# Contiguous first loads and a token-major, woven end in an attention and ReGLU kernel

## The chip, the cores and the metric

The kernel runs on one core of a Trainium2 chip. The metric is device time in microseconds. Runs of one kernel scatter by about 1 us here. So times are compared as means of several runs taken in the same rounds, and the traces are read beside them.

## The reference

Two parts in a row, four batches, 49152 tokens of 128 channels:

```python
# attention with spatially reduced keys, which are also the values
kv_pool = kv.reshape(B, H//4, 4, W//4, 4, C).mean(axis=(2, 4))   # 384x32 pixels -> 768 keys
k = v = kv_pool.reshape(B, -1, C) @ w_sr
x = softmax(q @ k.T / sqrt(C)) @ v                               # B = 4, 12288 queries each
# ReGLU: d_model 128, d_ff 1536
out = (maximum(x @ w_gate, 0) * (x @ w_val)) @ w_out
```

## The kernel before

It works in 96 tiles of 512 tokens, four tiles to a group. Per tile there are 6 score matmuls, 24 value matmuls of 129 columns, and 12 hidden blocks, each with a value, a gate and an output projection. TensorE (PE) does all of these; ScalarE (ACT) does the exponentials and copies the value projections; VectorE (DVE) multiplies gate and value into the hidden block `hT`. The output projection of tile k-4 runs beside the scores of tile k.

The parts that the change touches (cuts are marked with `# ...`):

```python
def q_load_plain(i0, i1):                    # called for (0, 2) and (2, 4), tiles of group 0
    q32 = work.tile([128, i1 - i0, NS, C], FP32, ...)
    nc.sync.dma_start(
        q32, q[0, 0 : GRP * T, :].rearrange("(p i s) c -> p i s c", p=128, i=GRP)[:, i0:i1]
    )
# ...
def out_proj(k, fb):
    if k == NT - 2:                          # token-major: hT is the stationary operand
        # ... four matmuls of 128 columns, one for each slice s of 128 tokens
        return
    nc.tensor.matmul(o_banks[k], wo16[:, fb, :], hTs[k][:, fb, :], ...)   # one of 512 columns

def out_turn(k):                             # channel-major result: turned in 32x32 blocks
    nc.vector.transpose(o_t, o_banks.pop(k))
    nc.gpsimd.tensor_scalar(o_sb..., o_t..., 1.0 / X_SCALE**2, None, op0=ALU.mult)
    # ... 4 stores of 64 KB for a tile; 16 of 16 KB in the first and the last group

def out_last(k):                             # the last tile, token-major
    o_ps = bank([128, 2, 128])
    for s in range(2):
        for fb in range(NFB - 1):
            out_add(k, fb, s, o_ps[:, s], fb == 0 and s == 0)
    for s in range(2):
        out_add(k, NFB - 1, s, o_ps[:, s], False)
    out_scale(k, nc.vector, slice(0, 2), o_ps)
    out_store(k, slice(0, 2))
    for s in range(2, NS):
        o_ps = bank([128, 1, 128])
        for fb in range(NFB):
            out_add(k, fb, s, o_ps[:, 0], fb == 0)
        out_scale(k, (nc.scalar, nc.vector)[s % 2], slice(s, s + 1), o_ps)
    out_store(k, slice(2, NS))
```

The kv of the first batch (three pairs of key chunks, 2 MB each, each pair in four loads or lines of 512 KB) and q's first megabyte come through one queue, SyncE's (SPq): one kv pair, the two loads of q, then two kv pairs.

The softmax here doesn't subtract the row's maximum and nothing guards it: scores larger than these inputs give would overflow.

## Time and profile before

| | before |
|---|---|
| time, median of 3 runs | 1035.74 us (1035.46 to 1036.62) |
| span in the profile | 1034.1 us |
| PE busy | 1023.5 us, 99% |
| value projections start (end of the start-up) | 30.92 us |
| last scale done | 1029.48 us |
| last store issued, landed | 1030.44, 1032.78 us |

The prediction below shows the lines. Two habits help in reading them. A PE row of 99% says that the middle of the run is full, so the two ends are to be looked at one microsecond at a time. And a transfer's "landing" is read in this text from the trace's completion counts: a transfer is shared by the 16 DMA engines, each of which reports once, and the landing is the sixteenth report (for kv's fourth line, in the trace of before, the first report came at 8.61 us and the sixteenth at 9.71).

### The profile page before, as it was taken

What the parts mean: (1) busy time and instruction counts of PE and PEld (TensorE: products, weight loads), DVE (VectorE), ACT (ScalarE), POOL (GpSimd) and SP (SyncE); (2) the same over time, 40 slices, a digit from 0 to 9 for tenths busy, and PEclk for the clock granted to TensorE, in tenths of its full rate; (3) what the DMA queues carried; (4) which work ended last, traced back from release to release, by engine and by line L of the source; (5) the groups of instructions that cost most, each with busy time, mean ns of one, the idle gap of its engine ahead of it and who ended that gap; (6) DMA issues with size and microseconds to landing.
All of it is one profiled execution on the core that took longest, in us unless ns stands there. A gap on an engine that the chain in (4) does not pass through costs nothing.

```text
span 1034.1 us, 19981 instructions
## 1 busy us (share of the span) xinstructions
PE 1023.5 (99%) x6540; PEld 543.3 (53%) x6540; DVE 910.6 (88%) x1669; ACT 909.6 (88%) x1749; POOL 281.4 (27%) x288
## 2 busy tenths in 40 slices
PE   8999999999999999999999999999999999999998
PEld 5555555555555555555555555555555555555554
DVE  3888889998989898998889898989898989888897
ACT  4988899888888889888888888888898888889986
POOL 1212146521211125642212121664121211111111
PEclk9999999999999999999999999999999999999999
DMA  8936396562543547736345157573652533513122
GB/s 292 133 57 74 84 198 144 83 92 43 82 67 50 80 120 161 169 53 89 55 64 88 31 86 151 142 161 57 82 78 42 78 60 56 86 31 67 31 46 48
DMA packets 330840, 93.34 MB, mean 90 GB/s; under 512 B 310768, under 2 KB 324080, under 8 KB 330736
## 3 DMA queue, kind: packets, MB, share of 16 engines
q1 hardware_dynamic: 315648, 78.76, 39.1%
q0 software_dynamic: 14944, 13.24, 10.6%
q8 instruction: 51, 0.84, 0.3%
q14 instruction: 53, 0.43, 0.2%
q10 hardware_dynamic: 144, 0.07, 0.0%
HBM read 53.94 MB, written 26.35 MB: 78 GB/s over the span
## 4 chain that ended last, share of the span: by engine, by line
PE 97%; DMA 2%; DVE 0%; SPq 0%; ACT 0%; issue 0%
PE bank_ps L278 24%; PE bank_ps L289 24%; PE bank_ps L313 24%; PE bank_ps L240 12%; PE bank_ps L229 12%; DMA parts<-in_kv_dram 1%; DMA q<-in_q_dram 1%; PE bank_ps L299 0%; PE bank_ps L188 0%; DVE hT L292 0%; SPq L138 0%; ACT aT L230 0%; PE bank_ps L162 0%; PE bank_ps L180 0%; SPq L100 0%
## 5 line engine op out<-in xcount | busy, mean ns | idle before, releaser
L292 DVE SCALAR_TENSOR_TENSOR hT<-bank_ps,val 128x512 f16<-128x512 f32 x1152 | 758.2, 686 | 91.6 <-ACT val L282 71.1
L282 ACT CAST val<-bank_ps 128x512 f16<-128x512 f32 x1152 | 678.7, 591 | 102.4 <-PE bank_ps L278 100.5
L278 PE MATMUL bank_ps<-xT,wv 128*128 128x512 f16 x1152 | 436.6, 379 | 0.1
L289 PE MATMUL bank_ps<-xT,wg 128*128 128x512 f16 x1152 | 436.6, 379 | 0.0
L313 PE MATMUL bank_ps<-hT,wo 128*128 128x512 f16 x1128 | 427.5, 379 | 0.0
L230 ACT ACTIVATE aT<-bank_ps 128x512 f16<-128x512 f32 x576 | 346.3, 605 | 0.9 <-PE bank_ps L229 0.8
L323 POOL TENSOR_SCALAR o_sb<-o_t 128x512 f32<-128x512 f32 x94 | 140.0, 1489 | 700.8 <-DVE rinv L248 673.3
L240 PEld LDWEIGHTS <-aT 128*128 128x128 f16 x2304 | 177.2, 98 | 133.4 <-issue 0.9
L240 PE MATMUL bank_ps<-kv,aT 128*128 128x129 f16 x2304 | 223.5, 220 | 0.5 <-DVE kv L198 0.4
L229 PE MATMUL bank_ps<-qT,kv 128*128 128x512 f16 x576 | 216.8, 379 | 0.4 <-DVE qT L121 0.2
L278 PEld LDWEIGHTS <-wv 128*128 128x128 f16 x1152 | 112.7, 98 | 133.6 <-issue 0.2
L289 PEld LDWEIGHTS <-wg 128*128 128x128 f16 x1152 | 112.7, 98 | 68.6 <-issue 0.2
L313 PEld LDWEIGHTS <-wo 128*128 128x128 f16 x1128 | 110.4, 98 | 67.2
L229 PEld LDWEIGHTS <-kv 128*128 128x128 f16 x576 | 56.1, 98 | 68.0 <-ACT kv L182 0.8
L256 DVE TENSOR_TENSOR x<-bank_ps,rinv 128x256 f16<-128x256 f32 x188 | 79.7, 425 | 6.6
L321 DVE STREAM_TRANSPOSE o_t<-bank_ps 128x512 f32<-128x512 f32 x94 | 66.4, 706 | 0.0
L85 POOL DMA_DIRECT2D q<-in_q_dram x88 | 48.4, 557 | 0.3 <-issue 0.3
L147 POOL TENSOR_TENSOR s<-parts 128x512 f32<-128x512 f32 x36 | 44.9, 1266 | 0.0
L248 DVE RECIPROCAL rinv<-bank_ps 128x2 f32<-128x2 f32 x192 | 28.0, 146 | 0.6 <-PE bank_ps L240 0.6
L149 POOL TENSOR_TENSOR s<-s 128x512 f32<-128x512 f32 x18 | 22.8, 1269 | 1.4
L151 POOL TENSOR_TENSOR c<-s 128x256 f32<-128x256 f32 x18 | 13.1, 728 | 1.4
L173 ACT COPY kvT<-bank_ps 128x128 f32<-128x128 f32 x4 | 1.1, 266 | 11.2 <-PE bank_ps L162 9.7
(53 smaller groups left out, 94.4 us busy)
## 6 DMA issues: line engine op xcount, KB each, us to landing
parts<-in_kv_dram SPq DMA_DIRECT2D x48, 512.0 KB, 6.6
out_dram<-o_sb SPq DMA_DIRECT2D x352, 64.0 KB, 2.2
q<-in_q_dram POOLq DMA_DIRECT2D x88, 128.0 KB, 4.4
out_dram<-o_sb SPq DMA_DIRECT2D x96, 16.0 KB, 1.5
xT<-x SPq DMA_TRANSPOSE x94, 2.4
placed<-blocks SPq DMA_DIRECT2D x9, 128.0 KB, 1.8
kvT<-placed SPq DMA_DIRECT2D x36, 32.0 KB, 1.9
q<-in_q_dram SPq DMA_DIRECT2D x2, 512.0 KB, 8.3
```

Source lines behind the costliest of these rows:

```text
L85: nc.gpsimd.dma_start(q16[32 * j : 32 * (j + 1)].rearrange("t (i s) c -> t i s c", i=GRP), rows[j])
L229: nc.tensor.matmul(s_ps, kv16[:, k // NST, jc, 0:C], qT_of(k), start=True, stop=True)
L230: nc.scalar.activation(aTs[k][:, jc, :], s_ps, AF.Exp, scale=qk_scale)
L240: nc.tensor.matmul(x_ps[:, i, :], aTs[k][:, jc, s * 128 : (s + 1) * 128], kv16[:, k // NST, jc, C : 2 * C + 1], start=(jc == 0 and i == 0) ...
L256: nc.vector.tensor_tensor(x16s[k][:, 2 * half : 2 * half + 2, :], x_ps[:, :, 0:C], rinv.to_broadcast([128, 2, C]), op=ALU.mult,)
L278: nc.tensor.matmul(va_ps, wv16[:, fb * 128 : (fb + 1) * 128], xTs[k], start=True, stop=True)
L282: nc.scalar.copy(val, va_ps)
L289: nc.tensor.matmul(g_ps, wg16[:, fb * 128 : (fb + 1) * 128], xTs[k], start=True, stop=True)
L292: nc.vector.scalar_tensor_tensor(hTs[k][:, fb, :], g_ps, 0.0, vals.pop((k, fb)), op0=ALU.max, op1=ALU.mult)
L313: nc.tensor.matmul(o_banks[k], wo16[:, fb, :], hTs[k][:, fb, :], start=fb == 0, stop=fb == NFB - 1)
L321: nc.vector.transpose(o_t, o_banks.pop(k))
L323: nc.gpsimd.tensor_scalar(o_sb.rearrange("t j s c -> t s j c"), o_t.rearrange("t (s j c) -> t s j c", s=NS, j=4), 1.0 / X_SCALE**2, None, ...
```

## The change

Its intent: read the first queries as two contiguous half megabytes instead of as interleaved 4 KB pieces, and shorten the end. "Token-major" means that a tile's result comes out with the tokens on the partitions, so it needs no turning and leaves in one store of 256 KB instead of sixteen of 16 KB. "Woven" means that the last tile's matmuls go through its four slices of 128 tokens in a mixed order, so that the first slices can be scaled and stored while the last are computed. Since the load then gives partition p the eight tokens 8p to 8p+7 of its half megabyte, the stores of the first four tiles get new addresses, in the same number and sizes.

```diff
-            q32, q[0, 0 : GRP * T, :].rearrange("(p i s) c -> p i s c", p=128, i=GRP)[:, i0:i1]
+            q32, q[0, i0 * T : i1 * T, :].rearrange("(p i s) c -> p i s c", i=i1 - i0, s=NS)
@@ out_proj
-        if k == NT - 2:
+        if k >= NT - 3:
@@ out_turn
-            if g in (0, NG - 1):
+            if g == 0:
+                to = rows.rearrange(
+                    "(e j t i s) (b c) -> e b i j t s c", e=2, j=4, t=32, s=NS, c=32
+                )
+                moves += [(to[k // 2, b, k % 2, j], o_b[:, j]) for j in range(4)]
+            elif g == NG - 1:
@@ out_last, whole body
+        parts = [bank([128, 2, 128]), bank([128, 1, 128]), bank([128, 1, 128])]
+        owns = [slice(0, 2), slice(2, 3), slice(3, 4)]
...   add(s, a, b): blocks a to b-1 of slice s; keep(n, engine): scale part n, then store it
+        held = NFB - 1
+        add(0, 0, held)
+        add(1, 0, held)
+        add(2, 0, held - 4)
+        add(0, held, NFB)
+        add(1, held, NFB)
+        keep(0, nc.vector)
+        add(2, held - 4, NFB)
+        keep(1, nc.scalar)
+        add(3, 0, NFB)
+        keep(2, nc.vector)
@@ main loop
-                if step == NFB - 1 and k < last:
+                if step == NFB - 1 and kO < NT - 3:
                     out_moves = out_turn(kO)
+                elif step == NFB - 1 and k < last:
+                    out_scale(kO, nc.vector, slice(0, NS))
+                    out_store(kO, slice(0, NS))
```

(A condition on group 0 in another load, which is never called for it, is left out.)

More of the change, by code (lines that the diff above doesn't have):

```diff
@@ L79, in q_load @@
         rows = q[b, n0 : n0 + GRP * T, :]
-        if g in (0, NG - 1):
+        if g == NG - 1:
             nc.gpsimd.dma_start(q16, rows.rearrange("(p s) c -> p s c", p=128))
@@ L333, in out_turn @@
             o_b = o_sb[32 * b : 32 * (b + 1)]
-            if g in (0, NG - 1):
+            if g == 0:
[4 more added lines that the diff above has]
+            elif g == NG - 1:
                 to = rows.rearrange("(j t i s) (b c) -> b i j t s c", j=4, t=32, s=NS, c=32)
@@ L361, in out_last, with add, keep @@
     def out_last(k):
+        parts = [bank([128, 2, 128]), bank([128, 1, 128]), bank([128, 1, 128])]
+        owns = [slice(0, 2), slice(2, 3), slice(3, 4)]
         o_banks[k] = None
-        o_ps = bank([128, 2, 128])
-        for s in range(2):
-            for fb in range(NFB - 1):
-                out_add(k, fb, s, o_ps[:, s], fb == 0 and s == 0)
-        for s in range(2):
-            out_add(k, NFB - 1, s, o_ps[:, s], False)
-        out_scale(k, nc.vector, slice(0, 2), o_ps)
-        out_store(k, slice(0, 2))
-        for s in range(2, NS):
-            o_ps = bank([128, 1, 128])
-            for fb in range(NFB):
-                out_add(k, fb, s, o_ps[:, 0], fb == 0)
-            out_scale(k, (nc.scalar, nc.vector)[s % 2], slice(s, s + 1), o_ps)
-        out_store(k, slice(2, NS))
+        def add(s, fb0, fb1):
+            n = max(s - 1, 0)
+            for fb in range(fb0, fb1):
+                out_add(k, fb, s, parts[n][:, s - owns[n].start], fb == 0 and s != 1)
+        def keep(n, engine):
+            out_scale(k, engine, owns[n], parts[n])
+            out_store(k, owns[n])
+        held = NFB - 1
[9 more added lines that the diff above has]
+        keep(2, nc.vector)
     ctx.enter_context(tc.manual_schedule())
```

## The prediction

> **What bounds the kernel now.** I read the page first, then the chain of waits, then the timelines of the first 35 us and the last 25 us, engine by engine. The page settles where a gain cannot come from:
>
> ```profile
> PE 1023.5 (99%) x6540; PEld 543.3 (53%) x6540; DVE 910.6 (88%) x1669; ACT 909.6 (88%) x1749; POOL 281.4 (27%) x288
> ...
> PE 97%; DMA 2%; DVE 0%; SPq 0%; ACT 0%; issue 0%
> ```
>
> TensorE (PE) is 99% busy and is 97% of the chain that ended last. In the middle, a pair of steps (six matmuls of 512 columns, one more for the scores, four of 129) takes 1.74 us, again and again. The change touches none of those matmuls. What is left to win lies at the two ends: before about 31 us, where PE waits for data, and after the last hidden block, where the result is written out.
>
> The start, in the chain of waits (start us, length us, what):
>
> ```profile
> 4.07 8.63 DMA q<-in_q_dram
> 12.69 0.02 issue
> 12.71 11.67 DMA parts<-in_kv_dram
> 24.38 0.14 issue
> 24.52 1.50 PE bank_ps L162 x12
> ```
>
> PE's work at 24.52 waits for the last line of kv. The stream before it is 2 MB of kv, 1 MB of q (the two loads that change), 4 MB of kv, all in one queue. By stretches of 1 us (columns: length, busy of five engines, clock, DMA share, GB/s):
>
> ```profile
> 7.00:8.00 1.00, 0.70 (x7) 0.46 (x5) 0.00 (x0) 0.00 (x0) 0.00 (x0) 1.00 1.06 340
> 8.00:9.00 1.00, 0.49 (x5) 0.50 (x6) 0.00 (x0) 0.00 (x0) 0.00 (x0) 1.00 1.01 324
> 9.00:10.00 1.00, 0.85 (x8) 0.61 (x7) 0.00 (x0) 0.00 (x0) 0.00 (x0) 1.00 1.00 287
> 10.00:11.00 1.00, 1.00 (x9) 0.82 (x8) 0.29 (x1) 0.12 (x1) 0.00 (x0) 1.00 0.98 336
> 11.00:12.00 1.00, 0.69 (x5) 0.39 (x4) 0.62 (x2) 0.42 (x3) 0.00 (x0) 1.00 1.03 422
> ```
>
> The DMA engines are busy throughout (share about 1), but move only 287 to 340 GB/s from 7 to 11 us and 422 after. The packets of 4096 bytes take 159 ns each when all is well and 189 to 228 ns on average in those four slices.
>
> The end, in the timelines of the store queue (SPq), PE and VectorE (DVE):
>
> ```profile
> 1019.96 9.43 SPq L535 DMA_DIRECT2D out_dram<-o_sb  x18
> 1029.49 1.35 SPq L352 DMA_DIRECT2D out_dram<-o_sb  x3
> ```
> ```profile
> 1025.92 0.72 PE L299 MATMUL bank_ps<-wo,hT 128*128 128x128 f16 x10
> 1026.86 2.30 PE L299 MATMUL bank_ps<-wo,hT 128*128 128x128 f16 x38 [0.21 <-DVE hT L292]
> ```
> ```profile
> 1019.57 7.83 DVE L292 SCALAR_TENSOR_TENSOR hT<-bank_ps,val 128x512 f16<-128x512 f32 x13
> 1027.91 0.42 DVE L349 TENSOR_SCALAR o_sb<-bank_ps 128x256 f32<-128x256 f32 x1 [0.51 <-PE bank_ps L299]
> 1029.19 0.29 DVE L349 TENSOR_SCALAR o_sb<-bank_ps 128x128 f32<-128x128 f32 x1 [0.86 <-PE bank_ps L299]
> ```
>
> The reader should see that the queue is still sending the small stores of the third last tile until 1029.39. The second last tile is ready at about 1027.0 and the first half of the last at 1028.33, yet all three large stores go out in a row from 1029.49. The last is issued at 1030.44, though its data was ready at 1029.48, and its completion count is full at 1032.78. The span ends at 1034.1.
>
> **What the Trainium skill says.** "DMA: Bandwidth & Descriptors", Rules for kernel authors, advises to coalesce small transfers. This trace agrees, in the queue's time: a 16 KB store holds the queue for 0.43 us and comes every 0.47, a 256 KB store of one piece to a partition holds it for 0.38. The same page, Latency and other measured facts, says that a row pitch of large powers of two (512 KiB and more) slows a copy, and infers channel aliasing. The pitch of q was 8 KiB and becomes 4, far below those; and the trace speaks against a penalty here: of the two loads of q, both with 8 KiB pitch, the first landed 1.70 us after the transfer before it, the second 1.28, and undisturbed kv loads of the same 512 KB land every 1.27 to 1.28. "TensorE: Matmul & The Clock Gate", on sustained spacing, gives about 81 ns for a matmul of 128 columns with its weight load; this trace has four in 0.22 us, 56 ns each, so I use that.
>
> **The change, part by part.**
>
> *Loads of q.* Each stays 128 pieces of 4096 bytes; only addresses change (tiles 0 and 1 from the first half megabyte, 2 and 3 from the second). The most there is to win: 4 us at 422 would have moved 1688 KB, 1287 came, so 401 KB or 0.95 us. But the dip starts at 7.2 us, when (by the completion counts) no DMA engine has reached q yet, and the second load of q is at full speed. What q itself shows is 1.70 - 1.28 = 0.42 us. I count 0.35 us, about that, partly discounted for the doubt and partly raised by a share of the dip before it. Would it reach the end? PE's start at 24.52 needs kv lines that landed at 23.14 and 24.38; each was held up by one DMA engine out of sixteen (the other fifteen were through at 21.65 and 22.89), on which an instruction fetch of 16 KB took 1.1 us from 20.98. Both move with what comes before, so I pass the 0.35 on in full. From 31 us PE is the bound and hands it on.
>
> *Third last tile token-major.* Removed: 12 matmuls of 512 columns, one VectorE transpose (0.71 us busy, 0.63 to the next instruction), one GpSimd scale (1.49, off the path), 16 stores. Added: 48 matmuls of 128 columns, one VectorE scale of 128x512, one store. PE: four small ones take 0.225 against 0.216, as the second last tile already shows with a step of 0.655 against 0.645; 12 steps, +0.1 us. It is hidden, since VectorE runs without a gap from 1011.8 to 1027.4 and sets when the last hidden blocks come. The scale: 0.42 us for 256 columns and 0.29 for 128, so 0.13 per 128 more, 0.69 for 512, against 0.71. Net on the path about -0.02. The queue: 16 stores are gone, from 1021.2 to 1029.4, so it stands free when the large ones come. This is the main gain.
>
> *Last tile woven, three stores.* PE stops at the 11th hidden block (the 10 matmuls at 1025.92, then a wait to 1026.86). In the new order the first run is again 11 blocks of slice 0, so it stops at the same place, and 1 + 11 + 7 + 2 + 5 + 12 = 38 matmuls follow, the same 38 as now. The weave wins PE nothing. It moves the ends: with 56 ns spacing and 0.22 for one, slices 0 and 1 are done after 21 matmuls (1028.2, now 1027.7), slice 2 after 26 (1028.5), slice 3 after 38 (1029.16, as now). Then: scale of the pair to 1028.65, store issued 1028.65 to 1029.03; scale of slice 2 on ScalarE to 1028.85, store to 1029.45; scale of slice 3 to 1029.48, store issued at 1029.5, which is 0.95 us earlier than 1030.44.
>
> *Landing of the last store.* Now 2.34 us from issue (1030.44 to 1032.78), behind 512 KB put in within a microsecond, at 316 to 393 GB/s. Then 64 KB, with only 192 KB near it. Yardsticks: the 16 KB stores land 1.5 us after issue, the 64 KB load of w_sr 1.8 (0.73 to 2.51). I take 1.8: 1029.5 + 1.8 = 1031.3, against 1032.78. Gain 1.5 us in all.
>
> *The stores of the first four tiles* keep their number and size; they are in mid-run behind PE: 0.
>
> Sum: -0.35 (start) - 1.5 (end) = -1.85. 1035.74 - 1.85 = **1033.9 us**.
>
> **The rivals.** (1) The start gives nothing, because the dip belongs to the time and not to the addresses: for it speaks the full-speed second half of q at the same pitch, and the slow packets before any q. Then about 1034.2. (2) The dip is q's alone and the whole 0.95 us comes back: for it, the dip ends as the first q load does. Then about 1033.3. The fetch on one engine could also fall elsewhere, worth up to 1.2 us either way (fifteen engines against the sixteenth); VectorE's adds and the kvT copies would eat part of it. (3) The end is eaten by a new wait: the scale of the third last tile now shares the three store buffers with the transposed tiles, and VectorE in the middle of its full stretch waits for stores of tile 90. Against it: those were issued some 20 us earlier. Or the bundle of three banks for the last tile waits for a reader; the order of instructions shows only waits for ScalarE and VectorE steps long over. If one bites, some 0.5 us is lost: 1034.4. (4) VectorE becomes more loaded: by its row lengths it does not.
>
> **Range and chances.** Start between -0.95 and +0.2, end between -1.1 and -1.8, the run-to-run spread of before 1.2 us (1035.46 to 1036.62). An eighty per cent range is 1032.9 to 1035.0. Two per cent is 20.7 us, which neither end has to give or take: same 0.99, and 0.005 to either side.
>
> **What would show it.** The small stores (now 32 of 16 KB after 1013) are 16, over by about 1021; five large stores, issued near 1020, 1027, 1028.7, 1029.1 and 1029.5 on the old clock, the last straight after its scale. PE has 38 matmuls after its stop at the 11th block. From the end of the last scale to the end of the span: 4.6 us now, 3.1 then. The q rows: first load landing 1.3 us after kv's fourth if addresses were the cause, still 1.7 if not; the first continuous PE stretch starting 0 to 0.9 us before 30.9. Wrong it would be if the last store still left late, if 64 KB took over 2.3 us to land, or if the start moved later.

## The result, and the profile after

| | before | after |
|---|---|---|
| time, median of 6 runs each | 1036.08 us | 1034.02 us (1032.81 to 1034.72) |
| mean of the same 6 runs | 1036.06 us | 1033.81 us |
| ratio | | 0.9978, 95% interval 0.9965 to 0.9991 |
| span in the profile | 1034.1 us | 1031.3 us |
| value projections start | 30.92 us | 29.69 us |
| last scale done | 1029.48 us | 1028.25 us |
| last store issued, landed | 1030.44, 1032.78 us | 1028.43, 1030.15 us |

A ratio is the mean time of one kernel's fast runs over that of the other's fast runs of the same rounds, so not quite the ratio of the two medians. It is by 2.1 to 2.3 us faster.

Lines have moved by some numbers in the file after: L279 is the value projection, L290 the gate, L300 the small output matmuls, L355 and L358 the scale and the store. The start, by the same stretches of 1 us as in the prediction (columns: length, busy of five engines, clock, DMA share, GB/s):

```profile
7.00:8.00 1.00, 0.78 (x8) 0.54 (x5) 0.00 (x0) 0.00 (x0) 0.00 (x0) 1.00 1.03 401
8.00:9.00 1.00, 0.55 (x5) 0.55 (x6) 0.00 (x0) 0.00 (x0) 0.00 (x0) 1.00 1.02 373
9.00:10.00 1.00, 0.83 (x9) 0.60 (x7) 0.00 (x0) 0.00 (x0) 0.00 (x0) 1.00 1.02 414
10.00:11.00 1.00, 1.00 (x10) 0.82 (x8) 0.29 (x1) 0.16 (x1) 0.00 (x0) 1.00 1.00 410
```

Where before moved 287 and 336 GB/s from 9 to 11 us, after moves 414 and 410. (From 7 to 9 us the traces of the study overlap, 332 to 379 GB/s with the old loads and 365 to 420 with the contiguous ones, so the difference seen there is not credited to the change.) The chain of waits (start, length, what) around 23 us has no DMA in it in this trace:

```profile
22.27 0.61 PE bank_ps L241 x8
22.89 0.43 PE bank_ps L230 x2
23.32 1.47 PE bank_ps L163 x12
```

PE goes from the scores straight on to the transposes of the last kv lines (L163), which before waited for a transfer until 24.38. Not every execution does: in the second trace of the changed kernel (after_again) PE waits 0.69 us for a kv line there, until 23.77.

The end, in the timeline of the store queue and in the chain of waits:

```profile
1019.23 1.41 SPq L553 DMA_DIRECT2D out_dram<-o_sb  x1
1020.74 8.09 SPq L358 DMA_DIRECT2D out_dram<-o_sb  x5
```
```profile
1024.36 0.53 issue
1024.89 0.69 DVE hT L293
1025.63 2.31 PE bank_ps L300 x38
1027.96 0.29 DVE o_sb L355
```

The small stores are over at 1020.64, and the five large ones go out at 1020.74, 1025.88, 1027.53, 1027.95 and 1028.43: the first as soon as the small ones are through, the next two as their data come, and the last two 0.33 and 0.18 us after theirs, each behind the store before it. PE still stops before the 11th hidden block, and still has 38 matmuls after the stop, in 2.31 us as before. From the end of the last scale to the end of the span it is 3.05 us (1028.25 to 1031.3), where it was 4.6.

### The profile page after: what moved, and what is told of

The parts are those of the page before. It is cut to its first block, busy times and chain, and to the rows that moved or that the text cites. A ratio compares the mean times of both kernels' runs of the same rounds, so it can differ in the third digit from the quotient of the medians.

```text
span 1031.3 us, 20034 instructions
## 1 busy us (share of the span) xinstructions
PE 1023.6 (99%) x6576; PEld 545.2 (53%) x6576; DVE 910.4 (88%) x1669; ACT 909.6 (88%) x1749; POOL 279.9 (27%) x287
## 4 chain that ended last, share of the span: by engine, by line
PE 98%; DMA 1%; ACT 0%; DVE 0%; SPq 0%; issue 0%
PE bank_ps L279 24%; PE bank_ps L290 24%; PE bank_ps L314 23%; PE bank_ps L241 13%; PE bank_ps L230 12%; DMA parts<-in_kv_dram 1%; PE bank_ps L300 1%; PE bank_ps L163 0%; PE bank_ps L189 0%; ACT aT L231 0%; DVE hT L293 0%; PE bank_ps L181 0%; SPq L139 0%; ACT kv L183 0%; PE bank_ps L119 0%
## 5 line engine op out<-in xcount | busy, mean ns | idle before, releaser
L279 PE MATMUL bank_ps<-xT,wv 128*128 128x512 f16 x1152 | 436.6, 379 | 0.1
L290 PE MATMUL bank_ps<-xT,wg 128*128 128x512 f16 x1152 | 436.6, 379 | 0.0
L314 PE MATMUL bank_ps<-hT,wo 128*128 128x512 f16 x1116 | 423.0, 379 | 0.0
L279 PEld LDWEIGHTS <-wv 128*128 128x128 f16 x1152 | 112.7, 98 | 132.2 <-issue 0.2
L290 PEld LDWEIGHTS <-wg 128*128 128x128 f16 x1152 | 112.7, 98 | 67.2 <-issue 0.2
L300 PEld LDWEIGHTS <-hT 128*128 128x128 f16 x144 | 10.1, 98 | 6.1 <-DVE hT L293 0.3
```

The source lines that it names most:

```text
L279: nc.tensor.matmul(va_ps, wv16[:, fb * 128 : (fb + 1) * 128], xTs[k], start=True, stop=True)
L290: nc.tensor.matmul(g_ps, wg16[:, fb * 128 : (fb + 1) * 128], xTs[k], start=True, stop=True)
```

## The experiments

Twelve runs: nine new kernels, two of them run twice, and the changed kernel again; all are set against the kernel before on the same chip. "Less than before" is the difference of the plain means of the fast runs of the same rounds. The two runs that are not in the table, q_pitch16 (1034.32 us) and q_pitch8_apart (1033.99 us), are single profiled executions in an unknown state, and are used for their traces alone.

| run | median us | less than before | ratio, 95% interval |
|---|---|---|---|
| q_only (4 fast runs of 5) | 1035.81 | 0.50 | 0.9995 (0.9981 to 1.0008) |
| q_again, the same kernel | 1035.84 | 0.10 | 0.9998 (0.9986 to 1.0011) |
| tail_only | 1034.70 | 1.55 | 0.9984 (0.9970 to 0.9998) |
| tail_again, the same kernel | 1034.08 | 1.80 | 0.9980 (0.9966 to 0.9994) |
| third_only | 1034.15 | 1.68 | 0.9983 (0.9971 to 0.9996) |
| weave_only | 1036.23 | -0.07 | 1.0000 (0.9988 to 1.0013) |
| after_again | 1033.46 | 2.46 | 0.9976 (0.9963 to 0.9988) |
| no_stop | 1033.84 | 2.26 | 0.9978 (0.9965 to 0.9990) |
| two_queues | 1033.65 | 2.40 | 0.9977 (0.9964 to 0.9989) |
| before_fill4 | 1036.31 | -0.31 | 1.0002 (0.9989 to 1.0016) |

What the traces show of the start, one execution each. "q step" is the time from the landing of kv's fourth line to that of the first load of q. "Packet" is the mean duration of the 4096-byte packets that start between 9 and 11 us, and GB/s is that stretch's rate. "Third" and "fourth" are landings of the last kv pair's lines. "Fetch" is the start of a 16 KB instruction fetch on one DMA engine. The last column is when the value projections start, from where on PE is the bound.

| trace | pitch of q | q step | packet ns | GB/s | third | fourth | fetch | value proj. |
|---|---|---|---|---|---|---|---|---|
| before | 8 KB | 1.70 | 207 | 311 | 23.14 | 24.38 | 20.98 | 30.92 |
| tail_only | 8 KB | 1.91 | 209 | 301 | 22.03 | 24.27 | 21.34 | 30.80 |
| third_only | 8 KB | 1.65 | 218 | 297 | 22.95 | 24.03 | 20.78 | 30.60 |
| weave_only | 8 KB | 1.57 | 217 | 301 | 23.09 | 24.17 | 20.93 | 30.74 |
| tail_again | 8 KB | 1.35 | 192 | 324 | 23.27 | 24.35 | 21.10 | 30.91 |
| before_fill4 | 8 KB | 1.56 | 207 | 303 | 21.36 | 23.84 | 21.23 | 30.38 |
| after | 4 KB | 1.27 | 160 | 412 | 21.19 | 23.15 | 20.69 | 29.69 |
| q_again | 4 KB | 1.28 | 160 | 410 | 21.33 | 23.20 | 20.90 | 29.84 |
| after_again | 4 KB | 1.27 | 160 | 416 | 20.93 | 23.64 | 20.71 | 30.17 |
| no_stop | 4 KB | 1.28 | 160 | 416 | 21.24 | 23.70 | 20.55 | 30.23 |
| two_queues | 4 KB | 1.28 | 162 | 414 | 21.78 | 23.03 | 21.09 | 30.30 |
| q_pitch16 | 16 KB | 1.27 | 162 | 410 | 22.04 | 23.29 | 21.25 | 30.56 |
| q_pitch8_apart | 8 KB | 1.63 | 220 | 293 | 21.75 | 24.06 | 21.12 | 30.59 |

### The loads of q alone: q_only and q_again

Edit: on the kernel before, the first hunk of the change and the addresses of the first group's stores; nothing else.

```diff
-            q32, q[0, 0 : GRP * T, :].rearrange("(p i s) c -> p i s c", p=128, i=GRP)[:, i0:i1]
+            q32, q[0, i0 * T : i1 * T, :].rearrange("(p i s) c -> p i s c", i=i1 - i0, s=NS)
```

> The kernel before with the contiguous loads of q alone (and the stores of the first four tiles that go with them). Theory (the addresses make the first load of q slow): the first load of q lands about 1.28 us after kv's fourth line instead of 1.70, every later landing is about 0.45 us earlier, and the time falls by 0.4 to 1.0 us (0.45 from the load, the rest from where the instruction fetch falls). Rival (the dip belongs to the moment, not to the addresses): the first load still takes about 1.7 us and the time moves by less than 0.2 us. The end is as before: last store issued about 0.95 us after its scale is done.

The first, profiled, execution took 6204.66 us and is set aside: PE was slow from its first matmul on (four score matmuls took 5.63 us, against 1.15), while the record says that the full clock was granted. The other four runs took 1035.26 to 1035.87.

> The contiguous loads of q alone, once more, since the profile of the first run fell on an execution with a TensorE some six times slower throughout. Theory: first load of q 1.27 us after kv's fourth line; landings after it about 0.45 us earlier than before; time 0.4 to 0.6 us below before on average (first try 0.5), single runs up to 1 us, by where the instruction fetch near 21 us falls. Rival (no gain): within 0.2 us of before.

The trace does what the theory says: the q step is 1.28 us, and the stretch from 9 to 11 us moves 410 GB/s.

```profile
9.00:11.00 2.00, 1.81 (x16) 1.39 (x13) 0.29 (x1) 0.01 (x1) 0.00 (x0) 1.00 1.01 410
```

Against the same stretch of the kernel before:

```profile
9.00:11.00 2.00, 1.85 (x15) 1.43 (x14) 0.29 (x1) 0.12 (x1) 0.00 (x0) 1.00 0.99 311
```

The time is less clear. The second try shows only 0.10 us, which misses the 0.4 to 0.6 expected and lies in the rival's range; over both tries nine runs have a mean of 1035.76 against 1036.03 for before, 0.27 us less, with a standard error of about 0.18. In the trace the value projections start 1.08 us earlier than in the trace of before, and PE keeps that lead until 686 us, where it loses 0.43 us at once. That is a second source of scatter, which the section on the middle takes up. A third is the end, where the expectation was missed too: the last store left 1.55 us after its scale (1028.84), not about 0.95. The store queue of q_again (timeline):

```profile
1019.80 9.54 SPq L540 DMA_DIRECT2D out_dram<-o_sb  x17
1029.43 1.36 SPq L357 DMA_DIRECT2D out_dram<-o_sb  x3
```

At the last value projection PE was still 0.63 us ahead of before, but the last store left at 1030.39, against 1030.44. One of the small stores held the queue for 1.70 us (1.07 in the trace of before, 1.51 in weave_only, 1.66 in before_fill4; why one takes so long is not known). With the old end it is this queue that the last store waits for, and not PE, so part of an early start can be lost in it. These are single traces: how much of the gain is lost so on average was not measured.

### The end alone: tail_only and tail_again

Edit: on the kernel before, all hunks but those of q's loads and the first group's addresses.

> The kernel before with the changes of the end alone (third last tile token-major, last tile woven, stores apart). Theory: from the end of the last scale to the end of the span 3.05 us instead of 4.6, so 1.4 to 1.5 us faster; the start is as before (first load of q 1.7 us after kv's fourth line). If start and end are independent, the gains of this run and of the q loads alone add up to the whole, about 2.1 us.

> The changes of the end alone, once more, for the mean of its gain and a further trace of the old loads of q. Theory: 1.4 to 1.6 us below before, and the first load of q lands 1.55 to 1.9 us after kv's fourth line; the value projections start at 30.6 to 30.9 us. Rival (loads of q do not matter): start as in after_again, 29.7 to 30.3.

Gains of 1.55 and 1.80 us, and in the trace of tail_only 3.06 us from the end of the last scale (1029.86) to the end of the span (1032.92). The start is as before in both. Of the expectations, the gains were missed on the high side (1.55 against 1.4 to 1.5, 1.80 against 1.4 to 1.6), and so was one q step: in tail_again the q step is 1.35 us, not 1.55 or more, though its packets are still slow (192 ns). The step is read on the slowest of 16 engines and moves with whichever engine that is; the mean packet and the rate from 9 to 11 us separate the two sets without an overlap, and are the better measure.

Do the parts add up? The changed kernel's eleven runs (after and after_again) have a mean of 1033.68, the ten of the end alone 1034.37: with the end in place, the loads of q are worth 0.69 us (standard error some 0.25). Alone they measured 0.27 (0.18). The traces, five a side (without before_fill4), have the value projections start at 30.79 on average with the old loads and at 30.05 with the new, 0.75 us. Between 0.3 and 0.7 us is what these runs support; they don't fix it closer. The parts (0.27 and about 1.7) add up to some 1.95, the whole measured 2.25 and 2.46; that the loads are worth more with the new end fits the store queue of q_again above, but with these errors it is not shown.

### Which part of the end: third_only and weave_only

Edit of third_only: token-major third last tile, the old last tile. Edit of weave_only: the new last tile, the old third last.

```diff
 third_only
-        if k == NT - 2:
+        if k >= NT - 3:
...                                  and the hunk in the main loop
 weave_only
...                                  the new body of out_last alone
```

> Third last tile token-major, the last tile as before (two stores of 128 KB). Theory (the queue of small stores is what made the last store late): nearly all of the end's gain is here, 1.1 to 1.4 us faster than before; the last store, 128 KB, is issued straight after its scale and lands some 0.1 to 0.3 us later than 64 KB do. Rival (the weave and the smaller last store bring the gain): less than 0.5 us faster.

> The last tile woven with three stores, the third last tile as before. Theory: the queue is busy with small stores until some 0.1 us after the last scale, then four large stores leave every 0.47 us, one more than before; the last is issued about 1.4 us after its data is ready and is only 64 KB, so the time is within 0.3 us of before. PE has the same 38 matmuls after its stop at the 11th hidden block. Rival (the weave shortens PE's end): 0.4 us or more faster.

third_only gains 1.68 us, as much as the whole end and more than the 1.1 to 1.4 expected; weave_only gains nothing (0.07 us slower). The gain of third_only lies behind the last scale, and not in the work that was taken off VectorE: its last scale was done at 1029.59 (1029.48 before), and from there to the end of the span it took 3.16 us instead of 4.60. The store queue of weave_only shows why (timeline):

```profile
1019.78 9.96 SPq L544 DMA_DIRECT2D out_dram<-o_sb  x18
1029.84 1.85 SPq L352 DMA_DIRECT2D out_dram<-o_sb  x4
```

The small stores of the third last tile hold the queue until 1029.74, and now four large ones wait behind it. The last slice's scale was done at 1029.30; its store left at 1031.29, 1.99 us later (1.4 was expected). In third_only the queue is free:

```profile
1019.63 2.48 SPq L538 DMA_DIRECT2D out_dram<-o_sb  x3
1022.21 7.78 SPq L352 DMA_DIRECT2D out_dram<-o_sb  x4
```

Its last store, 128 KB, left at 1029.66, 0.07 us after its scale (1029.59), and landed at 1031.53, 1.94 us after the scale. In tail_only, with the weave and a last store of 64 KB, the landing came 1.89 us after the scale. So the smaller last store is worth 0.05 us. It should have been worth more (64 KB landed 1.72 us after issue), but it left 0.17 us late, because the store of slice 2 was still holding the queue.

### The changed kernel again: after_again

No edit.

> The changed kernel again, as the measure for the next one and for a second profile. Theory: 1.9 to 2.2 us below before; start of the value projections between 29.7 (a fetch that hits late) and 30.5 us (a fetch that hits as before), not always 29.69; from the end of the last scale to the end of the span 3.05 us. Rival (the profile of after was typical): start at 29.7 again and over 2.5 us below before.

2.46 us less than before, which is over the 1.9 to 2.2 expected and under the rival's 2.5; 3.05 us from the last scale (1028.95) to the end (1032.0), and the value projections at 30.17, both as expected. The first profile of after, with 29.69, was one of its luckier executions: its time, 1033.10, was the second shortest of six. The 2.8 us between the two spans of the first pair of profiles overstate the change (2.25 and 2.46 us).

### PE's stop: no_stop, and the queue again: two_queues

Edits, on the changed kernel; two_queues has both.

```diff
 no_stop
-        held = NFB - 1
+        held = NFB - 2
         add(0, 0, held)
         add(1, 0, held)
-        add(2, 0, held - 4)
+        add(2, 0, held)
         add(0, held, NFB)
         add(1, held, NFB)
         keep(0, nc.vector)
-        add(2, held - 4, NFB)
+        add(2, held, NFB)
 two_queues, besides
-            out_store(k, owns[n])
+            out_store(k, owns[n], nc.scalar if n == 1 else nc.sync)
```

> The changed kernel with its last tile reordered so that PE does not stop: the first 10 hidden blocks of slices 0, 1 and 2, then the rest. Theory: PE's stop before the 11th block (about 0.3 us in after) is gone, the 48 matmuls run in 2.65 + 0.22 us from their start, the end is 0.25 to 0.4 us earlier than after. Rival (VectorE's last hidden block sets the end): no change, since the last 8 and 12 matmuls come after it anyway.

> The changed kernel without PE's stop, and with the store of slice 2 issued from ScalarE's queue, so that the last store finds its own queue free. From the start of PE's last gate matmul to the landing of the last store: 5.57 us in after, 5.44 in no_stop (there the last store left 0.34 us after its scale). Theory (the stores of the end stand in each other's way in one queue): the last store leaves within 0.1 us of its scale and lands 5.2 us after the last gate matmul, 0.35 us earlier than after; time 2.3 to 2.9 us below before. Rival (landing is bound by the transfers themselves): 5.4 us or more again.

PE's row of the last tile, in after, no_stop and two_queues (timeline; the row before it is the last gate matmul in all three, at 1024.57, 1025.79 and 1025.33):

```profile
1024.79 3.14 PE L300 MATMUL bank_ps<-wo,hT 128*128 128x128 f16 x48
```
```profile
1026.01 2.84 PE L300 MATMUL bank_ps<-wo,hT 128*128 128x128 f16 x48
```
```profile
1025.54 2.84 PE L300 MATMUL bank_ps<-wo,hT 128*128 128x128 f16 x48
```

The stop cost 0.30 us, and it is gone. From the last gate matmul to the landing of the last store it is 5.58 us in after, 5.44 in no_stop and 5.35 in two_queues. So no_stop kept half of what PE gave: the scale was done at 1029.18 but the store left at 1029.52, behind the store of slice 2. With that one on ScalarE's queue the last store left 0.03 us after its scale, but landed 1.94 us after its issue instead of 1.72, perhaps because it shared the DMA engines with the other, which had left at 1028.11 and landed only at 1030.51. The expected 5.2 us was missed by 0.15, and the rival's 5.4 too. In the times (2.26 and 2.40 us less than before) neither can be told from the changed kernel (2.25 and 2.46); a version that beats it clearly was not found.

### What in the loads of q is slow: q_pitch16 and q_pitch8_apart

Both are the changed kernel with other addresses of q, so with wrong inputs. (The record calls their outputs correct all the same; it means that this check would not notice wrong rows in the first four tiles of q.)

```diff
-            q32, q[0, i0 * T : i1 * T, :].rearrange("(p i s) c -> p i s c", i=i1 - i0, s=NS)
 q_pitch16
+            q32, q[0, 0:4096, :].rearrange(
+                "(p x i s) c -> x p i s c", x=4, i=i1 - i0, s=NS
+            )[2 * (i0 > 0)],
 q_pitch8_apart
+            q32, q[0, 0:4096, :].rearrange(
+                "(g p x i s) c -> g x p i s c", g=2, x=2, i=i1 - i0, s=NS
+            )[i0 // 2, 0],
```

> Wrong result on purpose: the changed kernel with each piece of q (4096 bytes to a partition) read at a pitch of 16 KB instead of 4 (8 before), the second load 8 KB further on. Theory (spreading the pieces is what makes the first load slow): the first load lands 1.6 us or more after kv's fourth line, against 1.27 with pitch 4 KB and 1.57 to 1.91 with 8 KB. Rival (it is the interleaving of two loads on the same 8 KB that hurts, or something else of pitch 8 KB): 1.3 us.

> Wrong inputs on purpose: the changed kernel with both loads of q at the pitch of before, 8 KB, but in separate megabytes, so that they no longer read the two halves of the same 8 KB. In the five traces with the old loads a 4096-byte packet starting between 9 and 11 us took 192 to 218 ns on average; with pitch 4 KB and with pitch 16 KB 160 to 162. Theory (pitch 8 KB is itself slow): 190 ns or more in that window, and 280 to 350 GB/s. Rival (the two loads disturb each other on the same 8 KB): 160 ns and over 400 GB/s.

The first row is q_pitch16, the second q_pitch8_apart:

```profile
9.00:11.00 2.00, 1.50 (x12) 1.27 (x13) 0.00 (x0) 0.00 (x0) 0.00 (x0) 1.00 1.02 410
```
```profile
9.00:11.00 2.00, 1.83 (x16) 1.42 (x14) 0.29 (x1) 0.00 (x0) 0.00 (x0) 1.00 0.99 293
```

The first theory fell: pieces spread at 16 KB move at 410 GB/s, as fast as contiguous ones, so spreading as such is not slow. The second theory held: with a pitch of 8 KB the stretch is slow (293 GB/s, 220 ns a packet) even when the two loads no longer share 8 KB. So the pitch of 8 KB itself is what the change removed, and contiguity is one of two ways shown here to do so, each of the two tests by one trace. Why 8 KB and not 16 is open. It is open also why the first of the two loads at that pitch is slower than the second: in q_pitch8_apart, as in before, the second lands 1.28 to 1.29 us after the first, and 11 to 13 us is at 418 GB/s (in the other old loads it lands 1.29 to 1.45 us after). What the fast packets are worth in time these two traces don't tell: their value projections start at 30.56 and 30.59 us, the one with fast packets no earlier. In it kv's fourth line, before any q, had landed only at 10.55, against 9.87.

### The instruction fetch: before_fill4

The prediction named a fetch of 16 KB that holds up one of the sixteen DMA engines near 21 us.

```diff
-    fill(8)
+    fill(4)
```

> The kernel before with 4 warming matmuls instead of 8, so that PE stands 8 instructions earlier in its stream and its instruction fetch near 21 us comes later. Theory: the fetch moves to about 21.9 us or later, the third line of the last kv pair lands near 21.7 instead of 23.1 and PE's wait before 24.5 us shrinks by 0.4 to 0.8 us, unless the cooler PE makes the first kv transposes slower, which shows in the duration of the 32 matmuls at 5 to 11 us. Rival (the fetch is triggered by time or by another engine): it stays near 21 us and nothing moves.

Inconclusive. (The warming matmuls are the ones without use that PE runs until its first data come.) The shorter warm-up did not delay the first kv transposes (the last ended at 10.64 us, at 10.84 before). The fetch came at 21.23 instead of 20.98, much less than expected and inside the scatter of the other traces (20.55 to 21.34). The third line did land at 21.36, PE's wait ended at 23.98 and the value projections started at 30.38, half a microsecond early. But the time was 0.31 us above before, and with the fetch hardly moved, as the rival said, the early third line cannot be credited to the edit.

Without an experiment of its own, the traces still say something about the fetch. They don't name the engine of a packet, but in eleven of the thirteen a kv packet of 432 to 441 ns starts as the fetch ends (22.06 us in before), then comes one of 344 to 429 ns, and then packets of some 160 ns, one after another, while the other engines run dry. So the engine with the fetch is the one that comes last, by the 1.03 to 1.11 us of the fetch and nearly half a microsecond in the two packets after it. In two_queues and q_pitch16 no such row follows: the fetch held up no kv there. In all five traces with contiguous loads and 8 warming matmuls the third line is out before the fetch can hurt it (20.93 to 21.78). In four of the five with the old loads it is caught (22.95 to 23.27). The fetch comes at nearly the same time in both sets; the lines come about 0.4 us earlier in one. The third line releases VectorE's adds for the last kv pair, so being on time by 0.4 us can be worth more than 0.4 us to PE. That the lateness matters so to PE is an argument from ten traces, and no run took the fetch away.

### The middle

PE's value projections in each trace can be laid against those of before, one by one. The lead or lag of a trace is constant to 0.02 us for hundreds of microseconds, but it jumps once in nine of the thirteen traces of normal speed: by 0.14 to 0.84 us at 685 to 687 us (q_again, after_again, tail_only, third_only, before_fill4, tail_again, two_queues, q_pitch16), by 0.68 at 182 us (no_stop). The kernel before in its only profile, after, weave_only and q_pitch8_apart do not jump. (At the very end, every trace with the token-major third last tile falls back by another 0.09 us.) In the trace of before, the store queue around that place (timeline):

```profile
682.04 4.32 SPq L95 DMA_TRANSPOSE qT<-q  x1
686.45 2.71 SPq L535 DMA_DIRECT2D out_dram<-o_sb  x4
```

In tail_only, the same queue and the PE row that waits:

```profile
681.83 5.73 SPq L95 DMA_TRANSPOSE qT<-q  x1
...
687.64 2.72 SPq L547 DMA_DIRECT2D out_dram<-o_sb  x4
...
688.14 0.39 PE L278 MATMUL bank_ps<-xT,wv 128*128 128x512 f16 x1 [0.31 <-DMA xT<-x]
```

The transpose of a whole group of queries holds the queue for 5.73 us instead of 4.32, and PE then waits for a transposed tile `xT`, which comes through the same queue. Of the eight traces that jump there, seven show this transpose at 5.63 to 6.33 us; two_queues, with the smallest jump (0.14), does not (4.19). A long one does not always delay PE: weave_only has 5.52 us without a jump, and no_stop, which had lost its lead before, 5.64. What makes it longer in one execution than in another is not known. The new loads and the old have it about equally often, so it is no part of the change; it is likely a part of why five runs of a kernel scatter by over a microsecond.

## Why the prediction was right

The prediction was 1033.9 us with 1032.9 to 1035.0; measured were 1034.02 (six runs) and 1033.46 (five). By its own steps:

- **What bounds the kernel.** Right: PE's middle did not change, and both gains lie at the ends.
- **The end, 1.5 us.** Right, with 1.55 and 1.80 us for the end alone, and 3.05 us from last scale to end of span where 3.1 was forecast. The cause is as named, the queue of small stores: third_only has all of it. The last store landed 1.72 us after issue; 1.8 was assumed. It left 0.18 us after its scale instead of at once, because the store of slice 2 stood before it. The prediction's own spacing of 0.47 us a store says as much: from 1028.65, the third store leaves at 1029.6 and not at 1029.5. The large store of the third last tile was expected near 1020 on the old clock and left at 1020.74 on the new one, after a last small store that held the queue for 1.41 us; that cost nothing.
- **The weave gives PE nothing.** Right: 38 matmuls in 2.31 us after the same stop, and weave_only gains nothing. That it costs nothing to VectorE is right too (0.68 us for the scale of 512 columns, 0.69 forecast, 0.71 for the transpose). The 0.1 us that the small matmuls cost PE is there (0.09), and hidden, as forecast: at VectorE's last hidden block after is 1.22 us ahead of before, all of its lead.
- **The start, 0.35 us.** The sum was near what was measured (0.27 alone, 0.69 with the new end), on the low side of it if the traces are followed (0.75). With values that far apart, that 0.35 lies between the two times is partly luck. The term of 0.42 us for the first load of q is what this pair of traces shows, 1.70 to 1.27; over five traces a side the step falls from 1.64 to 1.28, by 0.36. One argument inside the step failed: the claim that the trace speaks against a penalty of the pitch, because the second load at the same pitch was at full speed. q_pitch8_apart shows the penalty at 8 KB. And "both move with what comes before", said of the last two kv lines, leaves out that the fetch does not: its time stays near 21 us while the lines move, which is the likely reason for gains above 0.42 us; it was not tested.
- **The rivals.** (1) Nothing from the start: against it stand the traces, and 0.69 us with the end in place; the 0.27 us alone, with its error of 0.18, would not have ruled it out. (2) All of 0.95 us: not reached on average. (3) and (4), new waits at the end or a busier VectorE: neither came.

## What to carry to other kernels

When the last results leave through one in-order queue, count the stores still ahead of the last one: here sixteen stores of 16 KB, one every 0.47 us, kept the end back by some 1.5 us, and making them one was worth more than any reordering of the last matmuls. A reordering pays only if it fills the stop that is there; here the held-back block was the 12th and the stop was at the 11th. Where several loads feed a start-up, look at the packet durations inside a busy DMA stretch, try another pitch, and repeat the profile, since one trace of each side overstated this gain by up to half a microsecond.

## What the Trainium skill lacked or had wrong

- "DMA: Bandwidth & Descriptors", Latency and other measured facts, speaks of slow row pitches from 512 KiB up. Here pieces of 4096 bytes at a pitch of 8 KB ran at 293 to 324 GB/s, while 4 KB ran at 410 to 416 and 16 KB at 410. The mechanism was not found.
- The same page, Issuing engines are not separate DMA queues, calls the sequencer's time to initiate a DMA usually small relative to the DMA itself. At a kernel's end it is what counts: 0.47 us a store, against 1.5 us from issue to landing of 16 KB, so that 16 of them kept the last results back.
- "TensorE: Matmul & The Clock Gate", on sustained spacing, gives about 81 ns for a matmul of 128 columns with its weight load. Here 48 in a row, each with its own weight load, took 2.84 us: without the 0.22 us of a single one, about 56 ns each. The section has a figure of about 56 ns too, for a single matmul's gap, and calls it too low for a real stream; here it is the one that holds.
- No page says what an instruction fetch costs the data transfers beside it: 16 KB held one DMA engine for 1.03 to 1.11 us in these traces' start-ups, the two data packets after it took 0.34 to 0.44 us instead of 0.16, and the transfers queued on that engine landed up to 1.8 us after those of the other fifteen (tail_again, third line: 21.49 and 23.27).
- No page has an execution that is slow from end to end like q_only's first, 6204.66 us with TensorE some six times slower throughout, at a recorded full clock. It was seen once and is not explained.
